# The order of the first requests and the first TensorE instructions: x ahead of the convolution taps, and fewer fillers

## The chip, the cores and the metric

The kernel runs on one core of a Trainium2 chip. The metric is the device time of one execution in microseconds (us), the median of several executions. Each core has a matrix engine (TensorE, "PE" in the profile, its weight loads "PEld"), a vector engine (VectorE, "DVE"), an activation engine (ScalarE, "ACT"), GpSimd ("POOL") and a queue engine that only issues transfers (SyncE, "SP"). Transfers (DMAs) between the large memory and the on-chip memory are requested on the queues of SP, ACT and POOL. Matmul results go to eight banks of a small accumulator memory (PSUM).

## The reference

```python
# x: (8, 4096, 192), weight: (8 heads, 7 taps), w_in: (192, 2048), w_out: (2048, 192), beta: (2048,)
w = softmax(weight, axis=-1)
out[b, s, h, g] = sum over k of w[h, k] * x_pad[b, s + k, h, g]   # 6 zeros ahead of each sequence
h = out.reshape(32768, 192) @ w_in
g = h * sigmoid(beta * h)
result = g @ w_out
```

A causal convolution of seven taps along the sequence, one set of taps for each of eight heads, is followed by a two-layer network with a swish activation. Nearly all arithmetic is in the two matrix products.

## The kernel before, in words

The 32768 tokens are cut into two halves (index `s`, 16384 tokens each), which are worked on side by side: a step takes n tokens of each half. The steps begin small (128, 128 and 256 tokens, then three of 256 and two of 384) and have 512 tokens from then on. The 192 channels are split into three groups of 64 (`NK = 3`), so that the 64 channels of half 0 and the 64 of half 1 fill the 128 partitions. For a step, `mm1` or, in the first three steps, `mm1_pair` multiplies the convolved tokens with w_in (128 of the 2048 hidden units, a "chunk", at a time); ScalarE applies the activation from PSUM into `g`; and `mm2` multiplies g with w_out one step later. The swish is computed as Silu of beta times h, and the division by beta is folded into w_out (`scale_w_out`).

In the steady part the convolution is done on VectorE (lines 295 to 306) ahead of its step. The first 512 tokens of each half are convolved on TensorE instead: for each tap k a diagonal matrix `diag[:, k]` is built (`make_diag`, line 200), x is transposed on TensorE (`transpose_0`, line 216) and copied from PSUM to `xr` (`take_0`, lines 222 and 224), and `conv_0` (line 230) sums seven shifted products for each half. `evac_0` scales the sum by the reciprocal of the softmax sum and writes it as the input of the first product.

The order of work is the order of the code: `pin` keeps each instruction in program order on its engine, and each engine works through its instructions in order. The opening, which the change touches, goes as follows.

- SP asks for the taps (`weight`, 8 x 7 numbers, line 123), then for the half s = 0 of x's first block of 128 tokens (line 125), for beta (line 127) and for the second block of both halves (line 131, called on line 134). ACT asks for the half s = 1 of the first block (line 125), then loads its exponential table (line 139).
- GpSimd makes the selection matrix `sel` and the identity (lines 146 and 148) and then asks for w_in in six pieces (line 113, called on lines 150 to 152): columns 0 to 255, 256 to 639 and 640 to 1023 of each half of the hidden units, with the third and fourth block of x (line 131) between the fourth and the fifth request, and for w_out and more of x behind them.
- TensorE starts with fillers (`warm`, line 184): matmuls of a constant into a bank that nobody reads, nine of 256 columns and one of 128 (lines 186 and 187). Then come the matmul that spreads the taps over the partitions (line 191), three more fillers (line 192), the three transposes of the first block (line 216, called on line 246), eight fillers (line 248) and the first convolution.
- VectorE takes the maximum of the spread taps (line 193), ScalarE the exponential with its sum (line 196), and VectorE makes the seven diagonals (lines 202 and 249). ScalarE takes the transposed block to `xr` (line 247) and loads the table for Silu (line 256).
- After the first block's convolution TensorE transposes the second block and beta (lines 262 and 264) and begins step 0: eight pairs u = 0 to 7 of chunks (u, u + 8), each of six matmuls (line 326) and two activations (line 330). Pairs 0 and 1 need w_in's first pieces, 2 to 4 the second, 5 to 7 the third. Parts of the next blocks' convolutions stand behind most pairs (`first_tile`, line 502).

Of the kernel before, what the change touches and what calls it, by code (L numbers as in the profile page):

```python
# [19 lines left out]
def kernel(  # L20
# [9 lines left out]
    nc = tc.nc  # L30
# [15 lines left out]
    def pin(ins):  # L46

        return tc.keep_in_program_order(ins)
# [71 lines left out]
    xb0 = consts.tile([128, 2, NS, D], BF16, name="xb0")  # L120
    xb1 = consts.tile([128, 2, NS, D], BF16, name="xb1")
    taps = consts.tile([H, K], FP32, name="taps")
    pin(nc.sync.dma_start(out=taps, in_=weight))
    for s, eng in enumerate((nc.sync, nc.scalar)):
        pin(eng.dma_start(out=x0[:, 0, s, :], in_=xs[s, 0:128, :]))
    beta16 = consts.tile([NF, 128], FP32, name="beta16")
    pin(nc.sync.dma_start(out=beta16, in_=moe_beta.rearrange("(c p) -> c p", p=128)))
    HF = F // 2
# [29 lines left out]
    for s in range(NS):  # L158
        pin(nc.gpsimd.dma_start(out=xb1[:, :, s, :],
                                in_=xs[s, TILE:TILE + 256, :].rearrange("(b p) d -> p b d", p=128)))  # L160
# [21 lines left out]
    def warm(n, cols):  # L182
        for _ in range(n):
            pin(nc.tensor.matmul(idle[:, 0, 0:cols], ones[:, 0:128], ones[:, 0:cols], start=True, stop=True))

    warm(9, 256)
    warm(1, 128)
    cv0 = psum_h.tile([128, 2, TILE], FP32, name="ph")
    nmax = consts.tile([128, 1], FP32, name="nmax")
    tap_ps = cv0[:, 1, 0:K]  # L190
    pin(nc.tensor.matmul(tap_ps, sel.rearrange("h s g j -> h (s g j)"), taps, start=True, stop=True))
    warm(3, 128)
    pin(nc.vector.tensor_reduce(out=nmax, in_=tap_ps, axis=AX.X, op=ALU.max, negate=True))
    etap = consts.tile([128, K], FP32, name="etap")
    tsum = consts.tile([128, 1], FP32, name="tsum")
# [23 lines left out]
    def take_0(t, b, act=False):  # L219
        dst = xr[:, :, PAD + 128 * b:PAD + 128 * b + 128]  # L220
        if act:
            pin(nc.scalar.activation(dst, t, AF.Copy))
        else:
            pin(nc.vector.tensor_copy(dst, t))
# [20 lines left out]
    pb = po_banks()  # L245
    t = transpose_0(pa[0], x0, 0)
    take_0(t, 0, act=True)
    warm(8, 128)
    for k in range(2, K):
        make_diag(k)  # L250
    rsum = consts.tile([128, 1], FP32, name="rsum")
# [366 lines left out]
```

## Time and profile before

| what | value |
|---|---|
| median of 4 runs | 686.41 us (685.9 to 687.25) |
| profiled execution, device time | 686.32 us |
| its span, first to last instruction | 684.5 us |
| TensorE matmul busy | 679.9 us, 99% of the span |
| TensorE weight load busy | 460.8 us, 67% |
| VectorE busy | 550.5 us, 80% |
| ScalarE busy | 583.5 us, 85% |
| GpSimd busy | 14.5 us, 2% |
| transfers | 66.85 MB, mean 98 GB/s |

Busy time is time in which the engine worked on at least one instruction. Matmuls overlap and their ends are modelled, so that a busy TensorE is not one at its peak. The chain of the work that ended last is followed backwards, at each step to what released the instruction or to the one before it on its engine. Of this chain 97% is TensorE and 1% each are transfers and GpSimd. In a line of the timeline the columns are the start and duration in us, the engine, the source line, the operation, what it writes and reads, the count, and in brackets how long the engine had been idle before it and what ended that. "SPq" and "ACTq" are requests for transfers on these queues. All times in the traces count from the start of the span.

### The profile page before, as it was taken

How to read it: one execution, taken by the hardware profiler on the slowest of the kernel's cores; microseconds unless marked ns; L12 is line 12 of the kernel's file. 1: busy time of each engine (PE TensorE's matmuls, PEld its weight loads, DVE VectorE, ACT ScalarE, POOL GpSimd, SP SyncE). 2: the span in 40 equal slices, each digit the busy share in tenths (PEclk: the TensorE clock that was granted, in tenths of full speed). 3: DMA queues.
4: the chain of work that ended last, by engine and by line, in shares of the span. 5: the costliest groups of instructions: out<-in, count | busy, mean ns of one | idle time of the engine just before them, and what ended most of it. 6: DMA issues, size and time to landing. Idle time of an engine off the chain costs nothing.

```text
span 684.5 us, 27214 instructions
## 1 busy us (share of the span) xinstructions
PE 679.9 (99%) x12530; PEld 460.8 (67%) x12530; DVE 550.5 (80%) x886; ACT 583.5 (85%) x585; POOL 14.5 (2%) x26
## 2 busy tenths in 40 slices
PE   9999999999999999999999999999999999999998
PEld 7799887666666666666666666666666666666667
DVE  5999999999978889878889888889888889875112
ACT  7999999888888888888888888888888888888881
POOL 8000000000000000000000000000000000000000
PEclk9999999999999999999999999999999999999999
DMA  9643434444423344423344423344324343220223
GB/s 205 183 127 93 128 101 99 110 117 118 116 74 70 105 107 117 117 55 84 105 112 117 108 59 89 100 118 117 91 53 106 105 117 72 53 58 11 49 48 94
DMA packets 150418, 66.85 MB, mean 98 GB/s; under 512 B 113648, under 2 KB 149696, under 8 KB 150304
## 3 DMA queue, kind: packets, MB, share of 16 engines
q1 hardware_dynamic: 146992, 61.08, 34.9%
q0 software_dynamic: 3168, 3.93, 2.7%
q8 instruction: 98, 1.61, 1.0%
q14 instruction: 16, 0.13, 0.1%
q10 hardware_dynamic: 144, 0.10, 0.0%
HBM read 28.32 MB, written 25.17 MB: 78 GB/s over the span
## 4 chain that ended last, share of the span: by engine, by line
PE 97%; DMA 1%; POOL 1%; ACT 0%; issue 0%; DVE 0%; POOLq 0%
PE ph L344 47%; PE po L423 43%; PE po L377 4%; PE po L461 2%; PE ph L326 1%; DMA w_in_s<-in_moe_w_in_dram 1%; POOL w_in_s L113 0%; PE po L230 0%; ACT gp L330 0%; POOL xb L131 0%; PE po L216 0%; POOL sel L146 0%; DVE o_sp L383 0%; POOL ident L148 0%; POOLq L146 0%
## 5 line engine op out<-in xcount | busy, mean ns | idle before, releaser
L349 ACT ACTIVATE g<-ph,beta 128x1024 bf16<-128x1024 f32 (+2 forms) x528 | 556.8, 1062 | 81.3 <-PE ph L344 62.1
L344 PE MATMUL ph<-xc,w_in_s 64*64 64x512 bf16 (+3 forms) x5952 | 612.7, 368 | 0.0
L423 PE MATMUL po<-g,w_out_s 64*64 64x512 bf16 (+1 forms) x5568 | 580.2, 372 | 0.0
L344 PEld LDWEIGHTS <-w_in_s 64*64 64x64 bf16 (+1 forms) x5952 | 275.3, 104 | 125.7 <-issue 0.4
L423 PEld LDWEIGHTS <-w_out_s 64*64 64x64 bf16 x5568 | 289.8, 118 | 84.0
L304 DVE SCALAR_TENSOR_TENSOR acc<-xt,tapn,acc 128x512 f32<-128x512 bf16 (+2 forms) x450 | 311.0, 760 | 0.9
L440 DVE STREAM_TRANSPOSE o_sb<-po 128x512 f32<-128x512 f32 (+1 forms) x87 | 76.3, 877 | 112.0 <-PE po L423 112.0
L304 DVE SCALAR_TENSOR_TENSOR xc<-xt,tapn,acc 128x512 bf16<-128x512 bf16 (+2 forms) x90 | 63.9, 760 | 0.2
L87 DVE CAST xb<-xf 128x768 bf16<-128x768 f32 (+1 forms) x62 | 48.4, 823 | 0.0
L302 DVE TENSOR_SCALAR acc<-xt,tapn 128x512 f32<-128x512 bf16 (+2 forms) x90 | 40.9, 484 | 1.1
L377 PE MATMUL po<-w_out_s,g 64*128 64x192 bf16 x512 | 28.3, 243 | 0.0
L377 PEld LDWEIGHTS <-g 64*128 64x128 bf16 x512 | 23.5, 94 | 1.6
L383 DVE COPY o_sp<-po 128x192 f32<-128x192 f32 x28 | 9.0, 351 | 8.5 <-PE po L461 7.3
L326 PE MATMUL ph<-xcp,w_in_s 64*128 64x256 bf16 (+1 forms) x144 | 15.1, 306 | 0.4 <-DMA w_in_s<-in_moe_w_in_dram 0.2
L330 ACT ACTIVATE gp<-ph,beta 128x256 bf16<-128x256 f32 x32 | 12.7, 476 | 1.3 <-PE ph L326 0.9
L461 PEld LDWEIGHTS <-g 128*128 128x128 bf16 x128 | 10.5, 98 | 0.4 <-issue 0.4
L461 PE MATMUL po<-w_out_s,g 128*128 128x192 bf16 x128 | 10.7, 246 | 0.0
L330 ACT ACTIVATE g<-ph,beta 128x512 bf16<-128x512 f32 x16 | 9.6, 691 | 0.1
L326 PEld LDWEIGHTS <-w_in_s 64*128 64x128 bf16 x144 | 6.7, 94 | 4.1 <-issue 1.6
L377 PE MATMUL po<-w_out_s,gp 64*128 64x192 bf16 x128 | 7.6, 243 | 0.0
L230 PE MATMUL po<-xr,diag 64*128 64x384 f32 x49 | 7.5, 373 | 0.0
L377 PEld LDWEIGHTS <-gp 64*128 64x128 bf16 x128 | 6.0, 94 | 1.6
(52 smaller groups left out, 58.8 us busy)
## 6 DMA issues: line engine op xcount, KB each, us to landing
xf<-in_x_dram SPq DMA_DIRECT2D x60, 384.0 KB, 4.1
out_dram<-o_sb SPq DMA_DIRECT2D x108, 192.0 KB, 4.7
xt<-xb SPq DMA_TRANSPOSE x122, 3.1
out_dram<-o_sp SPq DMA_DIRECT2D x10, 192.0 KB, 4.3
w_out_f<-in_moe_w_out_dram POOLq DMA_DIRECT2D x4, 384.0 KB, 7.0
out_dram<-o_sb SPq DMA_DIRECT2D x8, 144.0 KB, 4.0
w_in_s<-w_in_s POOLq DMA_DIRECT2D x4, 192.0 KB, 6.8
out_dram<-o_sp SPq DMA_DIRECT2D x8, 96.0 KB, 1.9
```

Source lines behind the costliest of these rows:

```text
L87: pin((eng or nc.vector).tensor_copy(xbf_of[j][:, b0:b1, :, s, :].rearrange("p b k q -> p k b q"), xf_of[j][:, b0:b1, s, :].rearrange("p b ...
L302: pin(nc.vector.tensor_scalar_mul(a, src, w))
L304: pin(nc.vector.scalar_tensor_tensor(out=xc_of[i][:, k0:k1, o:o + m] if k == K - 1 else a, in0=src, scalar=w, in1=a, op0=ALU.mult, op1=ALU ...
L326: pin(nc.tensor.matmul(ph[:, h, 0:NS * n], w_in_s[half_of(h), kk, ts(fcs[h], 128)], xc_of[i][half_of(h), :, kk, :], start=(kk == 0), stop= ...
L330: pin(nc.scalar.activation(g_at(i, fcs[h])[:, :, 0:n], ph[:, h, 0:NS * n].rearrange("p (s t) -> p s t", s=NS), AF.Silu, scale=beta[:, fcs[ ...
L344: pin(nc.tensor.matmul(ph[m0:m1, s, n * e:n * e + n], w_in_s[half_of(s), kk, 128 * fc + m0:128 * fc + m1], xc_of[i][half_of(s), kk, 0:n], ...
L349: pin(nc.scalar.activation(g_at(i, fc)[:, :, 0:n], ph[:, :, n * e:n * e + n], AF.Silu, scale=beta[:, fc:fc + 1]))
L377: pin(nc.tensor.matmul(po[q][:, 0:D], g_at(i, fc)[r, s, ts(b, 128)], w_out_s[r, fc, :], start=(phase == 0 and fc == 0), stop=(phase == 1 a ...
L383: pin(nc.vector.tensor_copy(dst, po[:, 0:D]))
L423: pin(nc.tensor.matmul(po_of[i, m][half_of(s), 0:n], w_out_s[half_of(r), fc, m:D:NM], g_at(i, fc)[half_of(r), s, 0:n], start=(first and fc ...
L440: pin(nc.vector.transpose(osb_of[i][:, 0:n // L, :, m], po_of[i, m][:, 0:n].rearrange("p (b l) -> p b l", l=L)))
L461: pin(nc.tensor.matmul(po[:, 0:D], g_at(i, fc)[:, s, ts(b, 128)], w_out_s[:, fc, :], start=(fc == 0), stop=(fc == NF - 1)))
```

## The change

The taps move from the first place on SP's queue to the place behind x's half s = 1 on ACT's queue. SP's queue then begins with x's half s = 0. On TensorE the ten fillers ahead of the taps' matmul become six of 256 columns; the three between the taps' matmul and the transposes are taken out; and the eight behind the transposes become six. Nothing else changes its order on any engine: GpSimd's and VectorE's instructions stand as before, ScalarE's too apart from the added request.

```diff
@@ -120,9 +120,9 @@
     taps = consts.tile([H, K], FP32, name="taps")
-    pin(nc.sync.dma_start(out=taps, in_=weight))
     for s, eng in enumerate((nc.sync, nc.scalar)):
         pin(eng.dma_start(out=x0[:, 0, s, :], in_=xs[s, 0:128, :]))
+    pin(nc.scalar.dma_start(out=taps, in_=weight))
     beta16 = consts.tile([NF, 128], FP32, name="beta16")
     pin(nc.sync.dma_start(out=beta16, in_=moe_beta.rearrange("(c p) -> c p", p=128)))
@@ -183,13 +183,11 @@
-    warm(9, 256)
-    warm(1, 128)
+    warm(6, 256)
     cv0 = psum_h.tile([128, 2, TILE], FP32, name="ph")
     nmax = consts.tile([128, 1], FP32, name="nmax")
     tap_ps = cv0[:, 1, 0:K]
     pin(nc.tensor.matmul(tap_ps, sel.rearrange("h s g j -> h (s g j)"), taps, start=True, stop=True))
-    warm(3, 128)
     pin(nc.vector.tensor_reduce(out=nmax, in_=tap_ps, axis=AX.X, op=ALU.max, negate=True))
@@ -245,7 +243,7 @@
     t = transpose_0(pa[0], x0, 0)
     take_0(t, 0, act=True)
-    warm(8, 128)
+    warm(6, 128)
```

## The prediction

> **What bounds the kernel now.** I read the page's first two sections: TensorE is busy 679.9 of 684.5 us at full clock, in every slice. Only the opening, where TensorE still waits, can give time back, so I read the chain of the work that ended last, in order of time, for the first 34 us.
>
> ```profile
> 1.75 2.57 POOL w_in_s L113 x4
> 4.32 1.45 POOL xb L131 x2
> 5.77 0.61 POOL w_in_s L113
> 6.38 5.96 DMA w_in_s<-in_moe_w_in_dram
> 12.33 0.05 issue
> 12.38 0.39 PE ph L326 x4
> ```
>
> Columns: start, duration, what. The end of the run is traced back to 12.33 us, and there not to x or the taps, but to GpSimd's (POOL's) row of requests and its sixth one, half of w_in's last piece (columns 640 to 1023 of each half, line 150), issued at 6.38 and landed at 12.33. All of the first block's preparation (taps, transposes, first convolution) lies beside this. How late it could be is read from the waits between 8 and 34 us (total, times, longest):
>
> ```profile
> PEld L326 <- DMA w_in_s<-in_moe_w_in_dram: 0.7, 1, 0.7
> ...
> PE ph L326 <- DMA w_in_s<-in_moe_w_in_dram: 0.2, 1, 0.2
> ```
>
> TensorE stood ready for that piece (pair u = 5 of step 0): its weight load idled 0.7 us, its array 0.2 us. So an earlier opening waits longer here unless the piece comes earlier too. The timeline of the opening, where the change acts:
>
> ```profile
> 0.74 0.39 ACTq L125 DMA_DIRECT2D x<-in_x_dram  x1
> 0.74 0.41 SPq L123 DMA_DIRECT2D taps<-in_weight_dram  x1
> ...
> 0.78 2.19 PE L184 MATMUL ph<-const-bfloat16-1.0 128*128 128x256 bf16 x10 [0.78 <-PEq L602]
> ...
> 1.21 0.36 SPq L125 DMA_DIRECT2D x<-in_x_dram  x1
> ...
> 2.90 0.59 PE L191 MATMUL ph<-taps,sel 8*128 8x7 f32 x2
> ...
> 3.71 0.85 PE L216 MATMUL po<-ident,x 128*128 128x128 f32 x3
> ...
> 4.11 1.46 DVE L200 TENSOR_SCALAR diag<-ident,etap 128x128 fp32r<-128x128 f32 x7 [0.42 <-ACT etap L196]
> ...
> 4.59 0.49 ACT L222 ACTIVATE xr<-po 128x384 fp32r<-128x384 f32 x1 [0.52 <-PE po L216]
> ...
> 8.63 4.11 ACT L330 ACTIVATE gp<-ph,beta 128x256 bf16<-128x256 f32 x10 [0.54 <-PE ph L326]
> ```
>
> The taps' matmul runs behind ten fillers, then three fillers, then x's transposes; ScalarE copies these to xr, and the convolution (L230) begins at 5.34. From 8.63 ScalarE works through ten activations without a break (4.11 us), has idled 0.17 at 12.92 and 0.23 at 13.98, the late piece's cost to it, and runs on to 22.04. TensorE catches up with its second matmuls from then on.
>
> **What the Trainium skill says.** "TensorE: Matmul & The Clock Gate", section "What's actually happening": the array runs at half rate until about one busy window of 3413 ns; the windows run free of the kernel. The trace agrees: the L230 pairs start at 5.34, 5.83, 6.15, 6.45, 6.63, 6.81 and 6.99, thus 0.32 us apart and later 0.18; the trace's record of the grant is at 6.41. (The PEclk row shows no low clock before the first record, so I don't use it there.) "DMA: Bandwidth & Descriptors", "Issuing engines are not separate DMA queues": requests from several engines share the same 16 DMA engines, and only issue time is saved. The trace has that issue time: 0.36 to 0.43 us. The same page, "Queues, rings and completion order": a DMA engine takes turns between queues by packets. No view shows two x requests side by side, so I only take an upper bound from this.
>
> **The change part by part.**
>
> *Requests.* SP's first request was the taps (0.74); without it, x's half s = 0 moves from 1.21 to 0.74, beta from 1.62 to about 1.15, and x0's second block from 2.08 to about 1.61: 0.47 us each. On ScalarE's queue the taps follow x's half s = 1, at 0.74 + 0.42 = about 1.16, 0.42 later than before. Behind them stands the Exp table load (1.16 to 2.44), then at about 1.58 to 2.86, with its trial activation to 3.07; the real exponential comes after 3.3 (below), so this is hidden with 0.2 us to spare. No request of GpSimd moves; its first ones wait for its own selects (to 1.75).
>
> *Landings.* x's halves took 1.9 us each. Issued together, x is there at 0.74 + 1.9 = 2.64 if they don't disturb each other, and at 2.64 + 0.47 = 3.11 (where it is now) if all the stagger comes back as contention. TensorE's wait for the taps ran at 2.1 (its sequencer's semaphore row for L191), so they took at most 1.36 us: now 1.16 + 1.36 = 2.52 at best, and 1.16 + 1.9 = 3.06 if they come with x's packets ahead of them. I take 2.70, x also by then or shortly after.
>
> *Fillers.* Ten fillers end near 2.9; six of 256 columns, 0.213 us apart, end near 2.1. Then TensorE idles until 2.70, 0.6 us of the cold opening. The taps' matmul starts 2.90 - 2.70 = 0.20 earlier (bounds: 0.38 earlier, 0.16 later). Its maximum, exponential and first diagonals follow at the present distances (diagonals 1.21 after it): 3.91 instead of 4.11.
>
> *Transposes.* They can follow 0.53 us after the start of the taps' matmul, as the first filler does now (2.89 to 3.42). That is 3.23 instead of 3.71, 0.48 earlier (bounds 0.66 and 0.12). xr is taken at 4.11 instead of 4.59; ScalarE is then through with the exponential (3.52 to 3.88). Two diagonals are there by 4.4. The convolution begins at 5.34 - 0.48 = 4.86. Six fillers behind the transposes, 0.64 us, end near 4.5 and hold nothing up.
>
> *Convolution.* If the clock still comes at 6.41, the earlier pairs are cold: starts 4.86, 5.35, 5.67, 5.97, 6.29, then about 6.54 and 6.72, so the last is 6.99 - 6.72 = 0.27 earlier. Everything behind it, and ScalarE's row of activations, starts 0.27 earlier: 8.36 instead of 8.63. Pieces one and two of w_in are not yet waited for there.
>
> *The late piece.* If it lands at 12.33 as before, the 0.27 us are idled away before 12.38, and the gain is nothing. It can come earlier for one reason: x0's second block (192 KB) is asked for 0.47 us earlier, in a stretch in which the DMA engines are hardly used (18 to 61 GB/s from 2.7 to 3.6 us, by the DMA view of the first 12 us), and leaves the full stretch behind it emptier. At the 262 GB/s of 8.6 to 12.8 us its 192 KB are 0.73 us of transfer time; not more than 0.47 of this can move. So 0 to 0.47, of which at most 0.27 is of use. I take half of 0.27: 0.13 us.
>
> *Sum.* The profiled execution took 686.32 us, of which the span is 684.5 and 1.8 lies around it, untouched. 686.32 - 0.13 = 686.19. The runs' median is 0.09 above the profiled one: 686.28, so 686.3.
>
> **The rivals.**
>
> *The whole gain comes through.* If the piece moves as far as the opening, or is late in few runs, the ceiling is the opening's gain, 0.27, and with the best bounds (transposes 0.66 earlier, of which cold pairs leave some 0.18/0.32) 0.37; with 0.2 more if the wait at 12.38 goes altogether, about 0.5. 686.41 - 0.4 = 686.0. For: its last packets come 6.0 us after the request, a long tail. Against: the chain passes through it.
>
> *The clock comes later.* The 0.6 us gap breaks the window that lets the clock up; the place is TensorE from 6.41 on. One window later is 9.82 (the skill's 3.41 added to the trace's 6.41). The convolution then runs cold to its end, 0.35 us later than forecast; the first activations come at about 9.05, the conv pieces behind u = 1 finish near 10.3 instead of 9.6, and ScalarE ends its ten about 0.5 later, of which the wait at 12.38 covers 0.17: +0.35, 686.7. Slower in earnest needs a second window missed, to 13.2: each pair needs some 0.88 us of TensorE warm and twice that cold, so two pairs pass where four did, 2 x 0.88 = 1.7 more, 2.0 in all: 688.4. By 0.5 us lost per cold us past 9.82, it passes 0.2% at a grant near 11.9. For: the gap is new. Against: the window up to 6.41 begins at about 3.0 by the same page, after the gap, and is filled nearly as before.
>
> *The taps come late.* They stand behind 96 KB of x on one queue, and the in-order TensorE holds the transposes behind them. At 3.06 that leaves 0.12 of gain; only past 3.18 is the opening later than now, and the first 0.2 us of that are covered at 12.38. At 3.6: 3.6 - 3.18 = 0.4 later, less the 0.2 covered: 686.6.
>
> **How the numbers follow.** Forecast, gain mostly swallowed (686.1 to 686.5): 0.66. Whole gain (685.8 to 686.1): 0.12. Clock one window late, or taps late (686.5 to 687.1): 0.12. Clock two windows late: 0.05. The rest, 0.05, is for what I could not price, such as the tail of w_in's transfers in other executions. 0.2% is 1.4 us, about what a measurement of this kernel can tell from no change; only the last two cases reach it: slower 0.05 + 0.02, faster 0.03, within 0.90. The range takes in the forecast, the whole gain, and most of the small delays: 685.7 to 687.0.
>
> **What would show it.** Right: x's two requests both at about 0.74, taps' matmul near 2.7, transposes near 3.2, L230 near 4.9, the first gp near 8.4; and a wait of L326 for w_in that is longer than 0.7 on the weight load. Wrong: no such wait and ScalarE unbroken to the end of its gp row (whole gain); L230 pairs 0.32 apart to the last (clock late); taps' matmul past 3.2 (taps late). A time outside 685 to 687.8 would mean that the opening isn't what sets it.

## The result, and the profile after

| | before | changed |
|---|---|---|
| median | 686.37 us (685.41 to 687.29, 61 runs) | 687.17 us (686.65 to 687.84, 41 runs) |
| ratio to before, 95% interval | | 1.0012 (1.0007 to 1.0016) |
| profiled execution, its span | 686.32, 684.5 us | 687.83, 686.1 us |

The change makes the kernel 0.8 us slower. That is small, but beyond the interval, of the other sign than forecast, and 0.17 us above the range. The kernel before has two groups of times: 46 of its 61 lie from 685.41 to 686.87, and 15 from 687.09 to 687.29. The changed kernel's lie from 686.65 to 687.84, and its profiled execution is one of the slowest, so its profile shows more loss than the median. (Line numbers of the changed kernel are one or two lower from the fillers on.) Its timeline in the opening:

```profile
0.74 0.40 ACTq L124 DMA_DIRECT2D x<-in_x_dram  x1
0.74 0.40 SPq L124 DMA_DIRECT2D x<-in_x_dram  x1
...
0.78 1.44 PE L184 MATMUL ph<-const-bfloat16-1.0 128*128 128x256 bf16 x6 [0.78 <-PEq L600]
...
1.17 0.60 ACTq L125 DMA_DIRECT2D taps<-in_weight_dram  x1
1.19 0.43 SPq L127 DMA_DIRECT2D beta<-in_moe_beta_dram  x1
...
3.42 0.56 PE L190 MATMUL ph<-taps,sel 8*128 8x7 f32 x2 [1.20 <-DMA taps<-in_weight_dram]
...
3.91 0.91 PE L214 MATMUL po<-ident,x 128*128 128x128 f32 x3
...
5.40 0.69 PE L228 MATMUL ph<-xr,diag 64*128 64x384 f32 x1
...
9.85 5.00 ACT L328 ACTIVATE gp<-ph,beta 128x256 bf16<-128x256 f32 x12 [1.08 <-PE ph L324]
```

The requests moved as written. But the taps' matmul waits 1.20 us for the taps and begins at 3.42, 0.52 later than before, so the convolution begins at 5.40 (5.34 before). In this execution ScalarE's row of first activations then begins 1.22 us later. What happened between 5.40 and 9.85 is seen in the chain of the work that ended last:

```profile
1.17 2.11 DMA taps<-in_weight_dram
3.28 0.14 issue
3.42 0.56 PE ph L190 x2
3.98 0.84 PE po L214 x3
4.82 0.64 PE ph L184 x6
5.46 0.63 PE ph L228
6.08 0.32 PE ph L228
...
7.68 0.32 PE ph L228
8.01 0.84 PE po L214 x3
```

The chain no longer passes through GpSimd and w_in, but through the taps' transfer (2.11 us from request to landing) and TensorE. The convolution's pairs are 0.32 us apart to the last one: the array stays at half rate ("cold"; at full clock, 0.18 us apart, I call it "warm"). The trace's record of the grant of the full clock is at 10.27 us, 6.41 before.

The activations of the first two steps end at 23.25 us, 1.20 later than before (22.05). From there to the start of the last activation both kernels take 646.61 us. A second difference stands at the very end, between that activation and the final stage (L461, here L459); first before, then the changed kernel:

```profile
668.65 1.11 ACT L349 ACTIVATE g<-ph,beta 128x1024 bf16<-128x1024 f32 x1 [0.18 <-PE ph L344]
...
670.44 0.75 PE L461 MATMUL po<-w_out_s,g 128*128 128x192 bf16 x7
```

```profile
669.86 1.11 ACT L347 ACTIVATE g<-ph,beta 128x1024 bf16<-128x1024 f32 x1 [0.18 <-PE ph L342]
...
671.93 0.50 PE L459 MATMUL po<-w_out_s,g 128*128 128x192 bf16 x4
```

670.44 - 668.65 = 1.79 us before, 671.93 - 669.86 = 2.07 after: 0.28 more for the same products. I call this the late distance. Profiled time less the end of the first activations is 664.27 before and 664.58 after, so the medians' 0.80 us are about 0.3 at the end and 22.59 - 22.10 = 0.5 in the opening, if these two remainders hold in the other executions too.

### The profile page after: what moved, and what is told of

Its sections match the earlier page's. It is cut to its first block, busy times and chain, and to the rows that moved or that the text cites. A ratio compares the mean times of both kernels' runs of the same rounds, so it can differ in the third digit from the quotient of the medians.

```text
span 686.1 us, 27196 instructions
## 1 busy us (share of the span) xinstructions
PE 680.4 (99%) x12521; PEld 470.1 (69%) x12521; DVE 550.9 (80%) x886; ACT 583.3 (85%) x585; POOL 14.5 (2%) x26
## 4 chain that ended last, share of the span: by engine, by line
PE 99%; ACT 0%; DMA 0%; issue 0%; ACTq 0%; DVE 0%
PE ph L342 47%; PE po L421 43%; PE po L375 4%; PE ph L324 2%; PE po L459 2%; PE po L228 1%; ACT gp L328 0%; PE ph L228 0%; PE po L214 0%; DMA taps<-in_weight_dram 0%; PE ph L184 0%; PE ph L190 0%; ACTq L124 0%; DVE o_sp L381 0%; PE po L262 0%
## 5 line engine op out<-in xcount | busy, mean ns | idle before, releaser
L342 PE MATMUL ph<-xc,w_in_s 64*64 64x512 bf16 (+3 forms) x5952 | 592.6, 368 | 0.0
L421 PE MATMUL po<-g,w_out_s 64*64 64x512 bf16 (+1 forms) x5568 | 560.4, 372 | 0.0
L421 PEld LDWEIGHTS <-w_out_s 64*64 64x64 bf16 x5568 | 286.6, 118 | 82.0
L459 PEld LDWEIGHTS <-g 128*128 128x128 bf16 x128 | 10.5, 98 | 0.4 <-issue 0.4
L459 PE MATMUL po<-w_out_s,g 128*128 128x192 bf16 x128 | 10.7, 246 | 0.0
```

Source lines behind the costliest of these rows:

```text
L342: pin(nc.tensor.matmul(ph[m0:m1, s, n * e:n * e + n], w_in_s[half_of(s), kk, 128 * fc + m0:128 * fc + m1], xc_of[i][half_of(s), kk, 0:n], ...
L421: pin(nc.tensor.matmul(po_of[i, m][half_of(s), 0:n], w_out_s[half_of(r), fc, m:D:NM], g_at(i, fc)[half_of(r), s, 0:n], start=(first and fc ...
L459: pin(nc.tensor.matmul(po[:, 0:D], g_at(i, fc)[:, s, ts(b, 128)], w_out_s[:, fc, :], start=(fc == 0), stop=(fc == NF - 1)))
```

## The experiments

Theories: the *clock* theory (TensorE idles more in the opening, so the full clock is granted later), against the *taps* theory (the taps land behind x, and that delays the first block whatever the clock). The intervals of the ratios below come from the single times, and a ratio need not be the quotient of the two medians (e3). Where the edit is given against the kernel before or the changed one, the rest is as there.

**e1 to e4: each part alone, the gap filled, and no first fillers.**

```diff
 e1, against before: the two request lines of the change, no filler line
 e2, against before: the three filler edits of the change, no request line
 e3, against the changed kernel
-    warm(6, 256)
+    warm(12, 256)
 e4, against before
-    warm(9, 256)
-    warm(1, 128)
```

e1: 

> The requests are moved as in the change, the fillers stay as before. Clock theory (the fewer fillers let the full TensorE clock come a window later): the idle gap ahead of the taps' matmul shrinks to about 0.4 us, the convolution's pairs become 0.18 us apart before 7 us as before, and the time is within 0.3 us of before. Taps theory (the taps land 1.2 us later behind x, and this delays the first block): taps' matmul at 3.4 us as in the changed kernel, three fillers and the transposes behind it, convolution at about 5.6 to 5.7, and all or more of the 0.8 us is lost.

e2: 

> The requests stand as before (taps first), the fillers are those of the change. Clock theory: the clock is granted near 10 us instead of 6.4, convolution pairs 0.32 us apart to the last, 0.6 to 1.2 us slower than before. Taps theory: taps' matmul as early as 2.3 us, transposes as soon as x is there at 3.1, so the convolution starts near 4.9 and the time is the same as before or up to 0.3 us better.

e3: 

> The changed kernel with twelve fillers of 256 columns instead of six ahead of the taps' matmul, so that the 1.2 us gap until the taps land is filled. Clock theory: the grant is back near 6.4 to 6.7 us and the time falls by 0.6 to 1.0 us against the changed kernel, to about the time before. Taps theory: nothing is gained, 0.8 us slower than before as the changed kernel.

e4: 

> The kernel before without the ten fillers ahead of the taps' matmul; the three and the eight behind it stay. If each window of the clock gate is judged by itself and the one up to 6.4 us decides (it begins at about 3.0), nothing changes: grant near 6.4, time within 0.3 us of before. If activity before 3 us counts as well, the grant comes later, near 9.8 us, and the time is 0.6 to 1.2 us longer. Taps theory: taps' matmul at about 2.2 us instead of 2.9, nothing lost.

Measured: e1 687.45 us (ratio 1.0014, 1.0006 to 1.0023), e2 686.51 (1.0003, 0.9995 to 1.0011), e3 687.41 (1.0008, 1.0002 to 1.0015), e4 686.75 (1.0004, 0.9996 to 1.0012), before 686.47 beside them. By their medians e1, e2 and e3 are where the taps theory put them, and the clock theory missed all three; the traces and the single times show that the taps are not the whole of it. e1, with all its fillers, loses 1.0: convolution at 5.79, as the taps theory said, but the clock at 7.37. e2 has the late clock (8.84) without the loss, since its opening is really earlier:

```profile
2.23 0.56 PE L190 MATMUL ph<-taps,sel 8*128 8x7 f32 x2
...
3.35 0.88 PE L214 MATMUL po<-ident,x 128*128 128x128 f32 x3 [0.56 <-DMA x<-in_x_dram]
...
4.81 0.68 PE L228 MATMUL ph<-xr,diag 64*128 64x384 f32 x1
...
6.90 0.52 PE L228 MATMUL ph<-xr,diag 64*128 64x384 f32 x1
```

The convolution starts 0.53 us earlier and is cold to the start of its last pair, 6.90. The two nearly cancel. e4 is alike: its convolution starts at 5.01 and its clock comes at 8.68, which speaks for a part of the ten first fillers in the grant. e3 fell into two groups, 10 of 21 times from 685.8 to 686.9 and 11 from 687.4 to 687.8; its profiled execution is of the first, with the clock at 5.14. That led to a finer form of the clock theory: the window is free-running, so it stands differently in each execution, and an idle stretch spoils the windows that contain it.

**e5 to e8: both idle stretches filled, early taps kept busy, taps on SP's queue, and the number of requests.**

```diff
 e5, against the changed kernel
-    warm(6, 256)
+    warm(12, 256)
-    warm(6, 128)
+    warm(10, 128)
 e6, against before: warm(6, 256) ahead of the taps' matmul, warm(6, 128) and warm(7, 128) behind it and behind the transposes
 e7, against the changed kernel
-    pin(nc.scalar.dma_start(out=taps, in_=weight))
+    pin(nc.sync.dma_start(out=taps, in_=weight))
 e8, against before
-    pin(nc.sync.dma_start(out=beta16, ...
+    pin(nc.scalar.dma_start(out=beta16, ...
```

e5: 

> The changed kernel with both idle stretches filled: twelve fillers of 256 columns ahead of the taps' matmul and ten of 128 behind the transposes. Window theory (full clock is granted at the end of a free-running window of 3.41 us of which TensorE was busy for some 78% or more, so idle stretches shift the grant to a later window in part of the executions): no window from 0.8 us on fails, the grant lies between 4.2 and 7.6 us, the late group of the run before with twelve fillers (687.4 to 687.8) becomes rare, and the median falls to 686.2 to 686.6. Taps theory (what counts is only how late the taps' matmul is): taps at 3.4 us as in the changed kernel, 687.2.

e6: 

> The kernel before with its requests, six fillers of 256 columns ahead of the taps' matmul, six of 128 between it and the transposes and seven behind them, so that the taps' matmul comes as early as they land and TensorE is never idle. Window theory: the convolution starts near 4.8 us as with the fillers-only kernel and the clock is granted between 4.2 and 7.6 us: 685.6 to 686.1, 0.4 to 0.8 below before. If w_in's last piece binds instead (landing near 12.3 us), the gain ends at 0.1 to 0.2. Taps theory without the clock: 0.5 gained as well, so this run gives the size of the two together.

e7: 

> The changed kernel with the taps as SP's second request, behind x's half s = 0, instead of ACT's second. Taps theory: if ACT's queue was what delayed them, they land near 2.6 to 2.9 us and the opening gains 0.4; if it is x's packets ahead of them, they land at 3.2 as in the changed kernel. The last 24 products before the final stage take 0.29 us longer in all three profiles with moved requests than in the three without; if that comes from one request more on ACT's queue and one less on SP's, it is gone here (1.79 us from the last activation to the final stage), and the time is 0.3 below the changed kernel, 686.9.

e8: 

> The kernel before with beta's request on ACT's queue instead of SP's: the opening stays, the number of requests on the two queues is that of the changed kernel. If the number on the queues makes the late 0.29 us, the distance from the last activation to the final stage is 2.07 us and the time 0.3 above before, 686.7; if it is chance or has another cause, 1.79 us and no change.

Measured beside 686.51 before: e5 686.21 (0.9996, 0.9988 to 1.0005; no time above 686.95), e6 686.31 (0.9994, 0.9986 to 1.0002), e7 687.08 (1.0007, 0.9998 to 1.0015), e8 686.53 (0.9999, 0.9991 to 1.0008). e5 is the sharpest: fillers alone, with the taps no earlier, take back 1.0 us of the changed kernel's 687.2, where the taps theory expected nothing. 12 of its 13 times lie below the lowest of the changed kernel's 41 (686.65). Its timeline:

```profile
3.42 0.59 PE L190 MATMUL ph<-taps,sel 8*128 8x7 f32 x2
...
5.45 0.45 PE L228 MATMUL ph<-xr,diag 64*128 64x384 f32 x1
...
5.74 0.34 PE L228 MATMUL ph<-xr,diag 64*128 64x384 f32 x1
...
6.63 0.34 PE L228 MATMUL ph<-xr,diag 64*128 64x384 f32 x1
...
8.27 1.98 ACT L328 ACTIVATE gp<-ph,beta 128x256 bf16<-128x256 f32 x5 [0.54 <-PE ph L324]
```

Same taps' matmul (3.42), nearly the same start of the convolution (5.45), but warm pairs from 5.74 on: the last one starts 0.85 us earlier, and the activations begin at 8.27 instead of 9.85. e6's gain of 0.2 is half of the least that I expected, and its interval includes no change. In e7 the taps land at 3.27 as in the changed kernel, so it is x ahead of them, and not ACT's queue. Its late distance is 1.78, e8's 2.06, as expected of the count of requests, though no median shows this by itself.

**e9 to e12: taps first on ACT's queue, one instruction more on ScalarE, x in one request, and the changed kernel again.**

```diff
 e9, against the changed kernel: the taps' request on ACT's queue ahead of x's
 e10, against before
     pin(nc.scalar.activation(scrap, one, AF.Exp))
+    pin(nc.scalar.activation(scrap, one, AF.Exp))
 e11, against before: warm(6, 256), warm(3, 128), warm(7, 128), and
-    pin(nc.sync.dma_start(out=taps, in_=weight))
-    for s, eng in enumerate((nc.sync, nc.scalar)):
-        pin(eng.dma_start(out=x0[:, 0, s, :], in_=xs[s, 0:128, :]))
+    pin(nc.scalar.dma_start(out=taps, in_=weight))
+    pin(nc.sync.dma_start(out=x0[:, 0, :, :], in_=xs[:, 0:128, :].rearrange("s p d -> p s d")))
 e12: the changed kernel
```

e9: 

> The changed kernel with ACT's two requests exchanged: the taps first (0.74 us), x's half s = 1 second. Taps theory (x's packets ahead of the taps on the same DMA engines hold them up by 1.2 us, which costs the changed kernel the 0.5 us of opening that fewer fillers bring): taps land at 2.1, their matmul comes at 2.2, transposes at 3.2 to 3.4 when x is there, convolution at 4.8, as in the fillers-only kernel; with the late 0.29 us of one more request on ACT's queue the time is 686.7 to 686.9, 0.3 to 0.5 below the changed kernel. Rival (only the clock matters): 687.2, as the changed kernel.

e10: 

> The kernel before with one small activation more on ScalarE at the start (it repeats the trial of the exponential), requests unchanged. If one instruction more on ScalarE makes the late 0.29 us, the distance from the last activation to the final stage is 2.07 us and the time some 0.3 above before; if it is one request fewer on SP's queue or the request as such, 1.79 us and no change.

e11: 

> An attempt at a version better than both: the taps are ACT's only request, both halves of x's first block are SP's first, as one request; six fillers of 256 columns, three of 128 and seven of 128 keep TensorE busy. If one request of both halves lands at 2.7 to 3.0 us, the convolution starts near 4.5 and the time is 685.6 to 686.0; if it lands at 3.2 like the last half of before, it is as the early-taps kernel, 686.3. SP's queue has one request fewer and ACT's as many as before: the late 0.29 us stays away if ACT's queue makes it.

e12: 

> The changed kernel itself beside these, for a second profile. Window theory: its grant lies anywhere from 7.1 to 10.5 us, and the end of the first two steps' activations follows it; the taps land again at 3.2 to 3.3 and the late distance is again 2.07 us. 0.6 to 1.0 us slower than before.

Measured beside 686.42 before: e9 687.22 (1.0010, 1.0002 to 1.0018), e10 686.59 (1.0003, 0.9994 to 1.0011), e11 686.15 (0.9995, 0.9987 to 1.0003), e12 687.20 (1.0007, 0.9999 to 1.0015). e12 repeats the loss (0.78 by the medians), though in this smaller set its interval just includes no change; its taps land at 3.38 and its clock comes at 8.22. e9 missed: the taps land at 2.08, but now x's half s = 1, asked for at 1.35, lands only at 3.61 (2.26 us, against 1.94 for the first request on ACT's queue before), so the transposes begin at 3.74 and the convolution at 5.21. This is 0.13 earlier than before, and still the time is what the clock theory expected: the grant is at 9.49. e11's single request lands at 3.29, no earlier than the later half before; the convolution starts at 4.98. e10 shows the late distance with one activation and no request moved:

```profile
668.69 1.11 ACT L350 ACTIVATE g<-ph,beta 128x1024 bf16<-128x1024 f32 x1 [0.18 <-PE ph L345]
...
670.75 2.48 PE L462 MATMUL po<-w_out_s,g 128*128 128x192 bf16 x28
```

2.06 us. e10's execution also had its clock at 5.16 and its first activation at 8.11, and shows where an early opening goes (ScalarE's rows, then the wait for w_in):

```profile
8.11 4.10 ACT L331 ACTIVATE gp<-ph,beta 128x256 bf16<-128x256 f32 x10 [0.54 <-PE ph L327]
12.96 0.84 ACT L331 ACTIVATE gp<-ph,beta 128x256 bf16<-128x256 f32 x2 [0.75 <-PE ph L327]
```

```profile
PEld L327 <- DMA w_in_s<-in_moe_w_in_dram: 1.3, 1, 1.3
PE ph L327 <- DMA w_in_s<-in_moe_w_in_dram: 0.8, 1, 0.8
```

The 0.5 us by which it leads before are idled away at 12.96 (12.92 before).

**e13 and e14: both causes away with x still first, and the second idle stretch alone.**

```diff
 e13, against e7: warm(12, 256) and warm(10, 128) instead of warm(6, 256) and warm(6, 128)
 e14, against the changed kernel
-    warm(6, 128)
+    warm(10, 128)
```

e13: 

> The changed kernel with both causes taken away and x still first: the taps are SP's second request (so ScalarE's stream has no instruction more) and both idle stretches are filled (twelve fillers of 256 columns, ten of 128). If the loss is the sum of the two causes, 687.2 less 0.3 less 1.0 is 685.9, and the late distance is 1.79 us. If x's place ahead of the taps costs something by itself, 686.5 or more.

e14: 

> The changed kernel with ten fillers instead of six behind the transposes, the gap ahead of the taps' matmul left open. Window theory: every window that begins before about 3.2 us still contains the front gap and fails, so the grant lies between 6.6 and 10 us and the time is 0.0 to 0.3 below the changed kernel, 686.9 to 687.2. If the idle stretch behind the transposes is what counts, the time falls by 0.7 or more, to 686.5.

Measured beside 686.30 before: e13 686.66 (1.0009, 1.0000 to 1.0018; 7 of 13 from 686.0 to 686.7, the others from 687.0 to 688.8), e14 687.53 (1.0016, 1.0009 to 1.0023). e14 missed its range by 0.3: with the front gap left open, filling the second stretch gains nothing, and its fillers, cold, hold the convolution up (5.81). e13's median missed 685.9 by 0.8: a late group is there again, though e5, with the same fillers, had none in 13 runs.

All 16 profiled executions, in the order of their grant (us; the end of the first two steps' activations, and the late distance):

| kernel | grant | convolution starts | activations end | late distance |
|---|---|---|---|---|
| e5 | 4.91 | 5.45 | 21.61 | 2.06 |
| e3 | 5.14 | 5.44 | 21.48 | 2.07 |
| e10 | 5.16 | 5.28 | 22.09 | 2.06 |
| e13 | 5.21 | 5.58 | 21.83 | 1.79 |
| e8 | 6.38 | 5.34 | 22.09 | 2.06 |
| before | 6.41 | 5.34 | 22.05 | 1.79 |
| e6 | 6.56 | 4.91 | 21.69 | 1.79 |
| e11 | 6.74 | 4.98 | 22.26 | 1.78 |
| e14 | 7.22 | 5.81 | 22.47 | 2.08 |
| e1 | 7.37 | 5.79 | 22.51 | 2.07 |
| e7 | 7.89 | 5.39 | 22.53 | 1.78 |
| e12 | 8.22 | 5.50 | 22.65 | 2.06 |
| e4 | 8.68 | 5.01 | 22.51 | 1.78 |
| e2 | 8.84 | 4.81 | 22.31 | 1.78 |
| e9 | 9.49 | 5.21 | 22.84 | 2.07 |
| changed | 10.27 | 5.40 | 23.25 | 2.07 |

Each line is one execution. The eight kernels with a stretch of some 0.4 us or more without fillers ahead of the transposes, or with no first fillers, have the eight latest grants. In all 16 traces the record of the full clock lasts 675.84 or 679.25 us, 198 or 199 times 3.413 us, so here the clock changes only in steps of that length, and each execution has its own place for them. From the end of the first activations to the start of the last one all 16 take 646.61 us. From e3 to the changed kernel, with equal starts of the convolution, the grant is 5.13 us later and the end 1.77: about 0.35 us for each us of cold clock. The late distance is 2.06 to 2.08 in all nine executions with one instruction more on ScalarE and 1.78 or 1.79 in the other seven.

## Why the prediction was wrong, point by point

- **Requests and table load: right.** SP's requests at 0.74, 1.19 and 1.67; the Exp table and its trial activation end by 3.29, ahead of the exponential at 4.21. (They end 0.22 later than forecast: the taps' request took 0.60 us to issue, not 0.42.)
- **The landing of the taps: the first step that failed.** "I take 2.70", with 3.06 as the worst; it was 3.28, and 3.38 in e12. A request of 224 bytes that lands 1.35 us after its start when it is first took 2.1 us behind x's two halves, on either queue (e7: 3.27).
- **x by 2.70: failed too.** The semaphore records have x's halves at 3.25 and 3.45 (3.00 and 3.19 in e12), where before they were at 2.68 and 3.10. Asking for both at once gave no time back. TensorE did not have to wait for them here, since the taps' matmul stood ahead.
- **The opening:** a convolution 0.48 earlier became one 0.06 later. The fewer fillers would have brought 0.53 (e2); the moved requests took it away.
- **"If the clock still comes at 6.41": the step that cost most.** I set the window's start at about 3.0 for all executions and found the gap to lie before it. Grants at 10.27 and 8.22 in two executions of the same kernel show that there is no such fixed place. The Trainium skill says so in the very section that I cited ("TensorE: Matmul & The Clock Gate", "What's actually happening": the window is free-running), and the 16 grants, from 4.91 to 10.27, agree.
- **The clock rival:** its mechanism was right, its price (0.35 us) too small. It let the convolution start at 4.86 and the first activation come at 9.05. The convolution started 0.54 later, at 5.40, and from there to the first activation it was 4.45 us instead of 4.19, with the first products cold too (0.86 us from the start of the first of them to that activation, 0.67 before). So it came at 9.85, and the wait for w_in's last piece, counted on to cover 0.17, covered nothing: 1.20 us stayed to the end. In e12, whose 687.20 is near the median, the first activation came at 9.42 and 0.60 us stayed.
- **The late piece of w_in:** a true ceiling, but for an early opening only (e10); the changed kernel comes too late to meet it.
- **The end of the run, put at nothing: failed.** 0.28 us came there, from one instruction more on ScalarE.

Shown: filling both stretches takes 1.0 us from the changed kernel without earlier taps, and the 0.28 us follow the ScalarE instruction. Argued, with an estimate from all 16 traces (last section): that a share of busy time decides on a window. Still open: whether x's place ahead of the taps costs something besides (e13), and how the 0.5 us of opening divide exactly, since medians of 13 runs hang on where the windows fall. No version tried is faster than before beyond its interval. e11 is 1.05 us below the changed kernel beside it (e12), and e5 and e6 are 0.9 to 1.0 below it in other sets of runs. In e11's profile the lead over before (0.22 us) is not one of the opening, which ended 0.21 later, but comes after the last product (0.44, last section).

## What to carry to other kernels

Fillers that keep TensorE busy have a value of their own until the full clock is granted: count each idle stretch against every position of a free-running window, not against the one position that a single profile shows. When small requests are reordered in an empty queue, the one that now stands behind can pay more than issue time (the taps behind x 2.1 us instead of 1.35): ask which landing the first instruction then waits for. For effects below 0.1% take the phases apart by their own marks in the trace (grant, end of the opening, late distance); the medians alone would not have separated these causes.

## What the runs showed of the hardware that was not expected

- One instruction more at the start of ScalarE's stream, a request or a small activation, changes the end by 0.28 us, 650 us later. The traces show where it begins: one activation, the same in all nine such executions, starts 555.0 us after the end of the first two steps' activations, where it starts at 554.7 in the other seven, although TensorE's products up to there come at the same times within 0.01 us. First before, then the changed kernel (ScalarE's idle time in brackets):

```profile
576.77 2.35 ACT L349 ACTIVATE g<-ph,beta 128x1024 bf16<-128x1024 f32 x2 [0.24 <-PE ph L344]
```

```profile
578.26 2.12 ACT L347 ACTIVATE g<-ph,beta 128x1024 bf16<-128x1024 f32 x2 [0.53 <-PE ph L342]
```

  From 555.74 on (577.2 to 579.0 us in the traces) the matmul streams of 64 columns regroup in the nine: gaps of 0.03 and 0.18 us between pairs become others. In none of the other seven do they regroup. At the end 28 products with w_out are left behind the last one with w_in in the nine, 24 in the other seven, and the final stage starts 2.49 to 2.51 us after that one instead of 2.22, which is the 0.28 us. What holds that activation up was not found.
- Estimated from the timelines, a window that ends with a grant was busier than every window that did not. I count a matmul as busy until the next of its kind can start cold (0.213 us for a filler of 256 columns or a transpose, 0.107 for a filler of 128, 0.32 for a pair of the convolution, almost nothing for the taps' matmul). Then the 16 windows of 3.413 us ahead of the grants are 78% to 91% busy (before's 79%), and no earlier one is more than 76% (the changed kernel's, which ends at 6.85). By the profile's own busy time neither of these two has a gap, so the difference hangs on this way of counting. Slid over all positions, an edge of 76 to 78% gives a late grant in 16% to 30% of before's executions, 44% to 49% of e3's and 22% to 31% of e13's and e5's; late times were 15 of 61, 11 of 21, 6 of 13 and 0 of 13. Before, e3 and e13 fit this roughly, e5 badly.
- e11, with four requests on the hardware queues in the opening instead of five, needed 4.96 us from the start of its last product to the end of the execution instead of 5.40. I did not follow this up.
